# Routing with 18 small operations instead of 31, and GpSimd's scalings held until a turn's scores exist

## The chip, the cores and the metric

The kernel runs on one core of a Trainium2 chip. The metric is device time in microseconds (us), the median over runs. The core has several engines that work side by side, each through its own instructions in order: TensorE (PE, matmuls; PEld its weight loads), VectorE (DVE), ScalarE (ACT), GpSimd (POOL) and SyncE (SP), which here issues most transfers. They meet through semaphores: an instruction waits until others have got as far as it needs. Data lie in SBUF, and results of TensorE in the eight banks of PSUM.

## What is computed

A linear-attention layer (RWKV5) is followed by a mixture of experts with a cosine router, all in float32.

```python
B, H, S, D = 4, 8, 768, 48
for t in range(S):
    cur = einsum('bhd,bhe->bhde', u[None] * kt, vt)
    y[:, :, t] = einsum('bhd,bhde->bhe', rt, state + cur)
    state = w[None, :, :, None] * state + einsum('bhd,bhe->bhde', kt, vt)
x = y.transpose(0, 2, 1, 3).reshape(3072, 384)
# 8 experts, F = 1024
logits = (x / |x|) @ (emb / |emb|).T / tau
expert_idx = argmax(logits, axis=1)
gate_w = softmax(logits)[expert_idx]
for e in range(8):
    out[expert_idx == e] = gate_w * (relu(x @ w1[e]) @ w2[e])
```

Each of 3072 tokens goes to one expert. The router therefore makes, for each expert, a list of its tokens; the expert gathers those rows of x, and scatters its results.

## The kernel before

**Turns.** The sequence is cut into 6 chunks of 128 steps. A turn handles one chunk for two of the four batches (`u` = 0, 1), so there are 12 turns; turn t has chunk c = t // 2 and `bp` = t % 2. Within a chunk the recurrence becomes matmuls. GpSimd scales R and K by powers of the decay (`scale_r` L274, `scale_k` L270, tiles Rw and Kw), PE transposes them (`turn_in` L286), ACT copies them out of PSUM (`take_in` L290, tiles RT and KT). `scores` (L300) multiplies KT by RT into four banks D[0] to D[3], and DVE masks these into AT (`mask` L332). The diagonal gets its factor u from a second product: GpSimd makes KuT from KT (`own_k` L278), PE multiplies (`own_scores` L315), and DVE copies the diagonal into AT (`own_terms` L324). `outer` (L345) and `next_state` (L357) make the state after the chunk, `decay_state` (L363) scales it on GpSimd.

The outputs of a turn are made in the next one: `with_state` (L381) and `with_v` (L394) sum into banks Y[0] and Y[1], ACT copies them (`take_y` L401), PE transposes them into rows (`turn_y` L409), ACT copies the rows (`take_x` L413), SP stores them (`keep_x` L422), and ACT sums their squares (`squares` L428).

**Routing.** Every second turn a chunk is complete for all four batches. `logits` (L435) fills Y[0]; DVE copies it (`take_logits`), PE turns it (`turn_logits` L447), DVE copies it again (`keep_logits`). `choose_a` takes the root of the squares on GpSimd; `choose` (L469) divides the logits by the norm, finds the largest, makes a one-hot and running counts per expert; `exps` and `gate` make the weight; `ranks` (L505, PE) gives each token its rank among those of its expert, and `places` (L512), `places_b`, `put` and `collect` (L562) write its number and weight into that expert's list of up to 512. `choose`, `gate` and `places` have 31 small DVE operations a chunk. At the end `numbers_out` (L567) makes the list of row numbers, `take`.

**Order.** The order on every engine is written out by hand: `attention` (L579) gives each step a time within a plan, and the steps are emitted in the order of these times. They set nothing but the order, which all engines then follow. For turn t, `at` = t x PERIOD, `before` = a turn earlier, `nxt` = a turn later. Loads of K, R and V are planned three turns ahead on SP; the weights of the first two experts come on the same queue in turns 4 to 8.

**Experts.** After the turns, `experts` zeroes 8 row buffers G on GpSimd and gathers the rows of two experts into them (L665). Then for each expert PE transposes the rows (L678) and runs two layers (`layer1` L687, `layer2` L698).

The rest (`again`, `recur`, `slow_expert`) is for lists that overflow and for decays outside a range; it isn't entered with these inputs.

## Time and profile before

| | us |
|---|---|
| median of 3 runs | 576.18 |
| lowest and highest run | 575.48, 582.40 |
| the profiled execution | 575.27 |
| its span, first to last instruction | 573.4 |
| start of the first scores and of the last | 14.7, 176.9 |
| `take` ready | 206.2 |
| first matmul of the experts (L687) | 215.8 |

| engine | busy us | share |
|---|---|---|
| PE | 500.8 | 87% |
| PEld | 320.9 | 56% |
| DVE | 190.9 | 33% |
| POOL | 157.7 | 28% |
| ACT | 102.9 | 18% |

The profile is of one execution. The shares are over the whole span, of which the attention and routing take the first third and the experts the rest, so they say little on either stage. In the lists of the profile a row names the kernel's line, the engine, the operation and its tiles as out<-in, with partitions x elements; then the count and the time. A releaser is what an engine waited for.

### The profile page before, as it was taken

Reading aid. Unit: us, or ns where it says so; the run is one execution under the profiler, and the core shown is the slowest. Engines: PE = TensorE matmul, PEld = TensorE weight load, DVE = VectorE, ACT = ScalarE, POOL = GpSimd, SP = SyncE. Lnnn points to the kernel's source line nnn. Section 1 sums busy time; section 2 is a strip of 40 time slices with the busy share of each in tenths; the row PEclk is TensorE's granted clock in tenths of the full one; section 3 lists DMA queues with packets and bytes.
Section 4 is the critical chain, followed back from the end, with each engine's and each line's share of the span. In section 5 each row is a group of like instructions: output and inputs, shape, how many; then the busy total and the mean of one; then the engine's idle time right before and its main releaser. Section 6 shows DMA issues by size and latency. Waiting matters only on the chain.

```text
span 573.4 us, 9113 instructions
## 1 busy us (share of the span) xinstructions
PE 500.8 (87%) x3755; PEld 320.9 (56%) x3755; DVE 190.9 (33%) x423; ACT 102.9 (18%) x217; POOL 157.7 (28%) x186
## 2 busy tenths in 40 slices
PE   6799858597787639999999999999999999999990
PEld 3689757586776524554554554554554554554550
DVE  6576969779698520110110110110110110110001
ACT  2235503333043301101101101101101101101100
POOL 5676534535141244023023023023023020020020
PEclk9799969879699859999999999999999999999996
DMA  9966756937000112314314214314214213010010
GB/s 170 197 132 142 171 162 148 260 100 187 1 30 30 56 49 70 110 39 154 110 43 156 110 41 150 110 42 153 110 42 155 110 41 110 0 42 0 0 40 7
DMA packets 95510, 54.20 MB, mean 95 GB/s; under 512 B 78781, under 2 KB 90110, under 8 KB 95458
## 3 DMA queue, kind: packets, MB, share of 16 engines
q1 hardware_dynamic: 88658, 43.67, 27.9%
q0 software_dynamic: 4096, 9.45, 4.7%
q10 hardware_dynamic: 2704, 0.40, 0.4%
q8 instruction: 31, 0.51, 0.4%
q14 instruction: 21, 0.17, 0.1%
HBM read 45.63 MB, written 11.01 MB: 99 GB/s over the span
## 4 chain that ended last, share of the span: by engine, by line
PE 75%; DVE 15%; issue 2%; DMA 1%; ACT 0%; POOL 0%; DVEq 0%; POOLq 0%; ACTq 0%
PE ps L687 29%; PE po L698 29%; PE ps L300 4%; PE py L394 3%; PE py L381 2%; PE po L315 2%; PE py L678 2%; DVE AT L324 2%; PE ps L286 1%; DVE pre L488 1%; PE ps L345 1%; DVE xTe L679 1%; DVE P L549 1%; DVE oh L482 1%; DVE l L480 1%
## 5 line engine op out<-in xcount | busy, mean ns | idle before, releaser
L687 PE MATMUL ps<-xTe,w 128*128 128x512 f32 x384 | 166.5, 593 | 0.0
L698 PE MATMUL po<-w,hT 128*128 128x384 f32 x512 | 166.4, 486 | 0.0
L698 PEld LDWEIGHTS po<-w,hT 128*128 128x128 f32 x512 | 96.7, 190 | 66.2 <-issue 0.5
L687 PEld LDWEIGHTS ps<-xTe,w 128*128 128x128 f32 x384 | 73.1, 191 | 90.1 <-issue 88.3
L704 POOL DMA_INDIRECT out_dram<-y,take x32 | 31.7, 992 | 280.2 <-DVE y L703 276.1
L690 ACT ACTIVATE hT<-ps 128x512 f32<-128x512 f32 x64 | 38.2, 597 | 303.7 <-PE ps L687 303.7
L703 DVE TENSOR_SCALAR y<-po,lists 128x384 f32<-128x384 f32 x32 | 19.8, 618 | 165.5 <-PE po L698 165.5
L679 DVE COPY xTe<-py 128x512 f32<-128x512 f32 x24 | 15.9, 688 | 152.6 <-PE py L678 152.3
L324 DVE COPY_PREDICATED AT<-dmask,po 64x512 f32<-64x512 int32 x48 | 35.2, 734 | 8.3 <-PE po L315 7.6
L665 POOL DMA_INDIRECT G<-xs,take x32 | 32.6, 1020 | 18.4 <-DVE take L574 8.9
L300 PE MATMUL ps<-RT,KT 48*128 48x128 f32 x384 | 30.7, 322 | 6.6 <-ACT X L413 6.6
L332 DVE TENSOR_TENSOR AT<-ps,umask 128x512 f32<-128x512 f32 x48 | 30.0, 682 | 16.8 <-PE ps L300 16.8
L300 PEld LDWEIGHTS ps<-RT,KT 48*128 48x128 f32 x384 | 28.1, 229 | 9.2 <-ACT X L413 7.8
L401 ACT COPY YT<-py 128x512 f32<-128x512 f32 x24 | 12.9, 589 | 93.8 <-PE py L394 93.8
L363 POOL TENSOR_TENSOR T<-T,wC 128x384 f32<-128x384 f32 x10 | 8.3, 829 | 71.2 <-DVE inv L474 41.1
L278 POOL TENSOR_TENSOR KuT<-KT,uw 128x512 f32<-128x512 f32 x24 | 24.6, 1041 | 8.4 <-ACT KT L290 8.3
L274 POOL TENSOR_TENSOR Rw<-R,rpow 128x384 f32<-128x384 f32 x24 | 24.0, 1001 | 5.1 <-DVE wC L118 5.1
L394 PE MATMUL py<-AT,V 128*64 128x128 f32 x384 | 24.6, 283 | 0.0
L270 POOL TENSOR_TENSOR Kw<-K,kpow 128x384 f32<-128x384 f32 x24 | 24.2, 1010 | 0.0
L447 PE MATMUL py<-ident,lgT 128*128 128x128 f32 x6 | 2.4, 401 | 24.2 <-DVE lgT L443 24.2
L678 PE MATMUL py<-ident,G 128*128 128x128 f32 x96 | 15.6, 298 | 9.0 <-issue 5.2
L394 PEld LDWEIGHTS py<-AT,V 128*64 128x64 f32 x384 | 21.7, 142 | 1.1 <-issue 0.2
(152 smaller groups left out, 396.6 us busy)
## 6 DMA issues: line engine op xcount, KB each, us to landing
w<-in_moe_w_dram SPq DMA_DIRECT2D x24, 512.0 KB, 5.0
w<-in_moe_w_dram SPq DMA_DIRECT2D x32, 384.0 KB, 4.5
K<-in_k_dram SPq DMA_DIRECT2D x24, 192.0 KB, 3.4
V<-in_v_dram SPq DMA_DIRECT2D x24, 192.0 KB, 3.9
xs<-X SPq DMA_DIRECT2D x24, 192.0 KB, 2.1
R<-in_r_dram SPq DMA_DIRECT2D x22, 192.0 KB, 3.8
G<-xs,take POOLq DMA_INDIRECT x32, 3.6
out_dram<-y,take POOLq DMA_INDIRECT x32, 2.6
```

The lines of the kernel that those rows point to most:

```text
L270: k.nc.gpsimd.tensor_mul(of(k.Kw, t)[:, u, :, 0:D], of(k.K, t)[:, u], k.kpow)
L278: k.nc.gpsimd.tensor_mul(of(k.KuT, t)[:, u], of(k.KT, t)[:, u], k.uw[:, :, None].to_broadcast([128, NP, C]))
L300: k.nc.tensor.matmul(k.D[2 * u + par][:, p * C : (p + 1) * C], KT[rows, u, p, :], RT[rows, u, p, :], start=True, stop=True, skip_group_che ...
L324: k.nc.vector.copy_predicated(of(k.AT, t)[half, :, par].rearrange("q u (p i) -> q u p i", p=NP)[:, :, :, half], k.dmask[half, None, None, ...
L332: k.nc.vector.tensor_mul(of(k.AT, t)[:, u, par].rearrange("q (p i) -> q p i", p=NP), k.D[2 * u + par].rearrange("q (p i) -> q p i", p=NP), ...
L394: k.nc.tensor.matmul(y_out(k, par, p, u), V[:, u, 2 * p + par, :], AT[:, u, par, p * C : (p + 1) * C], start=c == 0 and u == 0 and q == 0, ...
L665: k.nc.gpsimd.indirect_dma_start(out=G[:, :], out_offset=None, in_=k.xs[:, :], in_offset=IndirectOffsetOnAxis(ap=k.take[:, e, t : t + 1], ...
L678: k.nc.tensor.transpose(ps[:, t * 128 : (t + 1) * 128], G[:, m * 128 : (m + 1) * 128], k.ident)
L687: k.nc.tensor.matmul(ps, w1[:, m, f * 128 : (f + 1) * 128], xT[:, m, :], start=(m == 0), stop=(m == NK - 1))
L690: k.nc.scalar.activation(hT[:, f, :], ps, ACT.Relu)
L698: k.nc.tensor.matmul(ps, hT[:, f, t * 128 : (t + 1) * 128], w2[:, f, :], start=(f == 0), stop=(f == NF - 1))
L704: k.nc.gpsimd.indirect_dma_start(out=k.out[:, :], out_offset=IndirectOffsetOnAxis(ap=k.take[:, e, t : t + 1], axis=0), in_=y[:, :], in_off ...
```

## The change

Seven things are edited.

1. `own_k` for the first half gets a dependency on the matmul of `scores` that was emitted last (`after`, `k.scored`). On GpSimd, in order, it stands ahead of the scalings for the next turn.
2. `choose` finds the largest among the logits as they are, and multiplies by the inverse norm only afterwards. The running counts over the four batches come from one scan over a tile `cum_oh` that holds the counts so far beside the one-hot; ACT copies the last count back. The small addition to the norm goes to GpSimd (`choose_a`).
3. `places` finds the tile of a rank by comparing it with 128, 256, 384, 512; the list's number and weight are laid side by side (`ng`), so that one product V of 32 elements and one QV of 256 take the place of Q and two QV of 128 each. V and QV move into `places_b`. `choose`, `gate`, `places` and V make 18 operations.
4. The lists start at SKIP, and numbers are stored less SKIP, so the last `collect` writes `take` itself; `numbers_out` goes.
5. The row buffers G are zeroed in turns 2 to 5.
6. The plan has other times: `own_k` after the scores of its own turn and not before, `decay_state` a turn later, `ranks` and `places` in the turn of `choose` and not in the next, `places_b`, `put` and `collect` in the turn after, where the next chunk's logits are made. The last two chunks have times of their own.
7. `turn_y` uses the banks D[0] and O[1] in this order, before O[1] and D[0]; `ranks` and `put` use other columns of Y[1].

```diff
-PERIOD = 10.0
+PERIOD = 11.2
...
+    k.ng = pool.tile([128, NCH, B, 2], F32, name="ng")
+    nc.vector.tensor_scalar_add(k.ng[:, :, :, 0], k.token, -float(SKIP))
...
+    k.level = numbers(k, "level", [128, TM], [[128, TM]], 128, 0)
+
+    k.cum_oh = pool.tile([128, E, B + 1], F32, name="cum_oh")
+    nc.vector.memset(k.cum_oh[:, :, 0:1], 0.0)
+    k.cum = k.cum_oh[:, :, 0]
+    k.oh = k.cum_oh[:, :, 1:].rearrange("q x b -> q b x")
+    k.on = pool.tile([128, E, B + 1], F32, name="on")
+    nc.vector.memset(k.on, 1.0)
+    nc.vector.memset(k.on[:, :, 0:1], 0.0)
+    k.back = pool.tile([128, NCH, B], F32, name="back")
+    k.rank = pool.tile([128, NCH, B], F32, name="rank")
+    k.lists = pool.tile([128, E, 2, TM], F32, name="lists")
+    nc.vector.memset(k.lists[:, :, 0, :], float(SKIP))
+    nc.vector.memset(k.lists[:, :, 1, :], 0.0)
+    k.take = pool.tile([128, E, TM], I32, name="take")
...
-    ps = k.bank[5].rearrange("q (g x) -> q g x", g=4)
+    ps = k.bank[1].rearrange("q (g x) -> q g x", g=4)
...
 def own_k(k, t, u):
-    k.nc.gpsimd.tensor_mul(
+    ins = k.nc.gpsimd.tensor_mul(
         of(k.KuT, t)[:, u], of(k.KT, t)[:, u], k.uw[:, :, None].to_broadcast([128, NP, C])
+    )
+    if u == 0:
+        after(k, ins, k.scored)
+
+
+def after(k, ins, other):
+
+    k.tc.add_manual_dep(
+        ins.ins, other.ins.name, mybir.DependencyInfo(mybir.DependencyClass.Sync, mybir.DependencyReason.DATA),
+        reason="turn",
     )
...
-            k.nc.tensor.matmul(
+            k.scored = k.nc.tensor.matmul(
...
 
 def choose_a(k, c):
+    ssq = k.ssq[c % 2]
+    k.nc.gpsimd.tensor_tensor(out=ssq, in0=ssq, in1=k.half, op=ALU.pow)
+    k.nc.gpsimd.tensor_scalar_add(ssq, ssq, 1e-6)
+
+
+def choose(k, c):
 
     nc, p = k.nc, k.rt
-    ssq = k.ssq[c % 2]
-    nc.gpsimd.tensor_tensor(out=ssq, in0=ssq, in1=k.half, op=ALU.pow)
-
-
-def choose(k, c):
-
-    nc, p = k.nc, k.rt
-    ssq = k.ssq[c % 2]
+    mx = p.tile([128, B], F32, name="mx", tag="mx")
+    nc.vector.reduce_max(mx, k.lg, axis=AX.X)
+    l = p.tile(FULL, F32, name="l", tag="l")
+    nc.vector.tensor_sub(l, k.lg, over_e(mx))
+    er = p.tile(FULL, F32, name="er", tag="er")
+    nc.vector.scalar_tensor_tensor(er, l, 0.0, k.rev[:, None, :].to_broadcast(FULL), ALU.is_equal, ALU.mult)
+    back = k.back[:, c, :]
+    nc.vector.reduce_max(back, er, axis=AX.X)
+    nc.vector.tensor_tensor(k.oh, er, over_e(back), ALU.is_equal)
+    k.counts = p.tile([128, E, B + 1], F32, name="counts", tag="counts")
+    flat = lambda a: a.rearrange("q x b -> q (x b)")
+    nc.vector.tensor_tensor_scan(flat(k.counts), flat(k.on), flat(k.cum_oh), 0.0, ALU.mult, ALU.add)
     inv = p.tile([128, B], F32, name="inv", tag="inv")
-    nc.vector.tensor_scalar_add(inv, ssq, 1e-6)
-    nc.vector.reciprocal(inv, inv)
-    l = p.tile(FULL, F32, name="l", tag="l")
-    nc.vector.tensor_mul(l, k.lg, over_e(inv))
-    mx = p.tile([128, B], F32, name="mx", tag="mx")
-    nc.vector.reduce_max(mx, l, axis=AX.X)
-    nc.vector.tensor_sub(l, l, over_e(mx))
-    oh = k.oh = p.tile(FULL, F32, name="oh", tag="oh")
-    nc.vector.scalar_tensor_tensor(oh, l, 0.0, k.rev[:, None, :].to_broadcast(FULL), ALU.is_equal, ALU.mult)
-    nc.vector.reduce_max(mx, oh, axis=AX.X)
-    nc.vector.tensor_tensor(oh, oh, over_e(mx), ALU.is_equal)
-    pre = k.pre = p.tile(FULL, F32, name="pre", tag="pre")
-    nc.vector.tensor_copy(pre[:, 0, :], k.cum)
-    for b in range(1, B):
-        nc.vector.tensor_add(pre[:, b, :], pre[:, b - 1, :], oh[:, b - 1, :])
-    nc.vector.tensor_add(k.cum, pre[:, B - 1, :], oh[:, B - 1, :])
+    nc.vector.reciprocal(inv, k.ssq[c % 2])
+    nc.vector.tensor_mul(l, l, over_e(inv))
     k.shifted = l
...
-    g = k.gates[:, c, :]
+    g = k.rt.tile([128, B], F32, name="g", tag="g")
     nc.vector.reduce_sum(g, k.shifted, axis=AX.X)
     nc.vector.tensor_scalar_add(g, g, 1e-9)
-    nc.vector.reciprocal(g, g)
+    nc.vector.reciprocal(k.ng[:, c, :, 1], g)
 
 
 def ranks(k, c):
     mm = k.nc.tensor.matmul
-    out = k.Y[1][:, 0 : B * E].rearrange("q (b x) -> q b x", b=B)
+    out = k.Y[1][:, 192 : 192 + B * E].rearrange("q (b x) -> q b x", b=B)
     mm(out, k.umask, k.oh, start=True, stop=False)
-    mm(out, k.ones, k.pre, start=False, stop=True)
+    mm(out, k.ones, k.counts[:, :, 0:B].rearrange("q x b -> q b x"), start=False, stop=True)
+    k.nc.scalar.copy(k.cum, k.counts[:, :, B])
...
+    full = p.tile(FULL, F32, name="full", tag="full")
+    nc.vector.tensor_mul(full, k.Y[1][:, 192 : 192 + B * E].rearrange("q (b x) -> q b x", b=B), k.oh)
+    r = k.rank[:, c, :]
+    nc.vector.reduce_sum(r, full, axis=AX.X)
+    wide = [128, B, TM]
+    over = p.tile(wide, F32, name="over", tag="over")
     nc.vector.tensor_tensor(
-        Q, k.slot[:, None, 0:width].to_broadcast(wide), e4[:, :, None].to_broadcast(wide), ALU.is_equal
-    )
-    k.QV = p.tile([128, B, 2, width], F32, name="QV", tag="QV")
-    nc.vector.tensor_mul(k.QV[:, :, 0, :], Q, k.number[:, c, :, None].to_broadcast(wide))
-    nc.vector.tensor_mul(k.QV[:, :, 1, :], Q, k.gates[:, c, :, None].to_broadcast(wide))
-    k.lo = lohi
+        over, r[:, :, None].to_broadcast(wide), k.level[:, None, :].to_broadcast(wide), ALU.is_ge
+    )
+    hi = p.tile([128, B], F32, name="hi", tag="hi")
+    nc.vector.reduce_sum(hi, over, axis=AX.X)
+    lo = k.lo = p.tile([128, B], F32, name="lo", tag="lo")
+    nc.vector.scalar_tensor_tensor(lo, hi, -128.0, r, ALU.mult, ALU.add)
+    nc.vector.tensor_tensor(
+        over, k.slot[:, None, 0:TM].to_broadcast(wide), hi[:, :, None].to_broadcast(wide), ALU.is_equal
+    )
+    k.at_tile = over
 
 def places_b(k, c):
-    P = k.P = k.rt.tile([128, B, 128], F32, name="P", tag="P")
+    nc, p = k.nc, k.rt
+    wide = [128, B, 2, TM]
+    V = p.tile(wide, F32, name="HV", tag="HV")
+    nc.vector.tensor_mul(
+        V, k.at_tile[:, :, None, :].to_broadcast(wide), k.ng[:, c, :, :, None].to_broadcast(wide)
+    )
+    wide = [128, B, E, 2 * TM]
+    k.QV = p.tile(wide, F32, name="QV", tag="QV")
+    nc.vector.tensor_mul(
+        k.QV, V.rearrange("q b j t -> q b (j t)")[:, :, None, :].to_broadcast(wide),
+        k.oh[:, :, :, None].to_broadcast(wide),
+    )
+    P = k.P = p.tile([128, B, 128], F32, name="P", tag="P")
...
+    new = k.Y[1][:, 128 : 128 + 2 * E * TM].rearrange("q (x j t) -> q x j t", x=E, j=2)
+    if c == NCH - 1:
+        k.nc.vector.tensor_add(k.take, k.lists[:, :, 0, :], new[:, :, 0, :])
+        k.nc.vector.tensor_add(k.lists[:, :, 1, :], k.lists[:, :, 1, :], new[:, :, 1, :])
+    else:
+        k.nc.vector.tensor_add(k.lists, k.lists, new)
...
-            plan.at(before + 0.0 + 2 * u, scale_r, k, t, u)
-            plan.at(before + 1.0 + 2 * u, scale_k, k, t, u)
+            plan.at(before + 3.0 + 2 * u, scale_r, k, t, u)
+            plan.at(before + 4.0 + 2 * u, scale_k, k, t, u)
             for which in range(2):
-                plan.at(before + 6.2 + 0.9 * u + 0.45 * which, turn_in, k, t, u, which)
-                plan.at(before + 6.6 + 1.2 * u + 0.6 * which, take_in, k, t, u, which)
-            plan.at(before + 8.0 + 1.1 * u, own_k, k, t, u)
+                plan.at(before + 7.4 + 1.4 * u + 0.45 * which, turn_in, k, t, u, which)
+                plan.at(before + 7.8 + 1.2 * u + 0.6 * which, take_in, k, t, u, which)
+            plan.at(at + 0.95 + u, own_k, k, t, u)
             plan.at(at + 0.9 * u, scores, k, t, u)
             for par in range(2):
                 plan.at(at + 1.0 + 1.4 * u + 0.7 * par, mask, k, t, u, par)
-        plan.at(at + 2.65, own_scores, k, t)
+        plan.at(at + 3.2, own_scores, k, t)
...
         if c < NCH - 1:
-            plan.at(at + 5.3, outer, k, t)
-            plan.at(at + 6.8, next_state, k, t)
-            plan.at(at + 7.2, decay_state, k, t)
-        plan.at(nxt + 1.75, with_state, k, t)
-        plan.at(nxt + 3.55, with_v, k, t)
+            plan.at(at + 6.4, outer, k, t)
+            plan.at(at + 7.4, next_state, k, t)
+            plan.at(nxt + 7.0, decay_state, k, t)
+        plan.at(nxt + 2.0, with_state, k, t)
+        plan.at(nxt + 4.4, with_v, k, t)
         for par in range(2):
-            plan.at(nxt + 5.3 + 0.6 * par, take_y, k, t, par)
+            plan.at(nxt + 6.4 + 0.6 * par, take_y, k, t, par)
         for u in range(2):
-            plan.at(nxt + 8.1 + 0.45 * u, turn_y, k, t, u)
-            plan.at(nxt + 9.1 + 0.6 * u, take_x, k, t, u)
-            plan.at(nxt + 9.2 + 0.6 * u, keep_x, k, t, u)
-            plan.at(nxt + 10.2 + 0.7 * u, squares, k, t, u)
-        if bp == 1:
-            plan.at(nxt + 9.0, logits, k, c)
-            plan.at(nxt + 9.5, take_logits, k, c)
-            plan.at(nxt + 9.8, turn_logits, k, c)
-            plan.at(nxt + 10.8, keep_logits, k, c)
+            plan.at(nxt + 9.7 + 0.45 * u, turn_y, k, t, u)
+            plan.at(nxt + 10.2 + 0.6 * u, take_x, k, t, u)
+            plan.at(nxt + 10.3 + 0.6 * u, keep_x, k, t, u)
+            plan.at(nxt + 11.4 + 0.7 * u, squares, k, t, u)
+        if bp == 1 and c < NCH - 1:
+            plan.at(nxt + 8.5, logits, k, c)
+            plan.at(nxt + 9.4, take_logits, k, c)
+            plan.at(nxt + 10.6, turn_logits, k, c)
+            plan.at(nxt + 10.9, keep_logits, k, c)
             then = nxt + P
+            plan.at(then + 2.9, choose_a, k, c)
+            plan.at(then + 7.9, choose, k, c)
+            plan.at(then + 9.3, exps, k, c)
+            plan.at(then + 9.72, ranks, k, c)
+            plan.at(then + 9.8, places, k, c)
+            plan.at(then + 11.0, gate, k, c)
+            last = 7.9 if c < NCH - 2 else 0.0
+            plan.at(then + P + last, places_b, k, c)
+            plan.at(then + P + (10.5 if c < NCH - 2 else 0.2), put, k, c)
+            plan.at(then + P + (11.0 if c < NCH - 2 else 0.3), collect, k, c)
+    end = NCH * 2 * P + 6.4
+    c = NCH - 1
+    plan.at(end + 1.3, logits, k, c)
+    plan.at(end + 1.4, take_logits, k, c)
+    plan.at(end + 5.0, turn_logits, k, c)
+    plan.at(end + 5.1, keep_logits, k, c)
+    plan.at(end + 5.9, choose_a, k, c)
+    for i, fn in enumerate((choose, exps, ranks, places, gate, places_b, put, collect)):
+        plan.at(end + 6.0 + i, fn, k, c)
     plan.at(-P + 0.4, load_small, k)
     plan.at(6.2, build_embeddings, k)
     plan.at(P + 6.2, decays, k)
+    for i, G in enumerate(k.G):
+        plan.at((2 + i // 2) * P + 7.5, k.nc.gpsimd.memset, G, 0.0)
     for e in range(2):
...
-    k.G = []
-    for i in range(8):
-        G = k.gp1.tile([128, DM], F32, name=f"G{i}")
-        nc.gpsimd.memset(G, 0.0)
-        k.G.append(G)
...
-    numbers_out(k)
...
-    n.rows, n.sums = (n.O[1], n.D[0]), n.D[0]
+    n.rows, n.sums = (n.D[0], n.O[1]), n.D[0]
...
+    n.G = [n.const.tile([128, DM], F32, name=f"G{i}") for i in range(2 * TM)]
```

## The prediction

> **What bounds the kernel now.** First the page: its span and the 40 slices of 14.3 us.
>
> ```profile
> span 573.4 us, 9113 instructions
> ...
> PE   6799858597787639999999999999999999999990
> ...
> DVE  6576969779698520110110110110110110110001
> ...
> POOL 5676534535141244023023023023023020020020
> PEclk9799969879699859999999999999999999999996
> ```
>
> From slice 15 on TensorE is full: the experts, whose instructions the change leaves as they are. Only the first 210 us can move, and there PE has holes, DVE is busiest, and the granted clock dips. So I cut that stretch at the starts of the scores (L300), 14.73, 26.81, 37.72, 48.20, 59.95, 78.46, 94.02, 112.87, 128.29, 147.13, 162.50 and 176.88, one per turn 0 to 11, and asked for busy time per engine. Columns: window and length, busy us and instructions of PE, PEld, DVE, ACT, POOL, then clock, DMA share, GB/s.
>
> ```profile
> 37.72:48.20 10.48, 10.00 (x217) 9.20 (x217) 6.19 (x10) 6.02 (x16) 8.64 (x10) 1.00 0.74 168
> ...
> 94.02:112.87 18.85, 11.81 (x253) 10.66 (x254) 16.91 (x35) 6.25 (x16) 10.39 (x11) 0.94 0.97 250
> 112.87:128.29 15.42, 14.12 (x225) 13.48 (x224) 10.25 (x19) 4.15 (x10) 3.97 (x5) 0.74 0.44 107
> ```
>
> Turn 2, without routing, takes 10.48 us. With routing a pair takes 34.3: in turn 6 DVE works 16.9 of 18.85 us, in turn 7 the clock is 0.74. The chain of waits says how:
>
> ```profile
> 108.58 0.93 DVE lohi L529
> ...
> 111.61 0.60 DVE P L549
> 112.21 0.21 DVE lgT L443
> 112.42 0.04 issue
> 112.47 0.47 PE py L447
> 112.94 3.72 PE ps L300 x32
> ```
>
> `places` runs ahead of the logits copy on DVE, `turn_logits` waits behind it on PE (6.1 us idle), and the scores then run at half clock: 3.72 us against 1.99 at 48.27. The timeline shows why DVE is slow:
>
> ```profile
> 125.15 2.04 POOL L278 TENSOR_TENSOR KuT<-KT,uw 128x512 f32<-128x512 f32 x2 [0.19 <-ACT KT L290]
> 125.25 0.98 DVE L480 TENSOR_TENSOR l<-l,mx 128x32 f32<-128x32 f32 x1
> ...
> 126.27 0.96 DVE L482 SCALAR_TENSOR_TENSOR oh<-l,rev 128x32 f32<-128x32 f32 x1
> 127.27 0.19 DVE L483 TENSOR_REDUCE mx<-oh 128x4 f32<-128x32 f32 x1
> ```
> ```profile
> 184.79 0.19 DVE L480 TENSOR_TENSOR l<-l,mx 128x32 f32<-128x32 f32 x1
> 185.02 0.20 DVE L482 SCALAR_TENSOR_TENSOR oh<-l,rev 128x32 f32<-128x32 f32 x1
> ```
>
> At 185 us, GpSimd idle, the same two operations take a fifth: beside a GpSimd scaling each ends when the scaling ends. Reductions (0.19) and operations that read PSUM are not held (the 48 masks span 0.67 to 0.69).
>
> **The change, part by part.** S is the end of a turn's scores and S+2.2 means 2.2 us later; durations are those of before's rows, with its 0.1 from one engine's end to another's start.
>
> *The hold.* `own_k` now waits for the last score emitted before it. Its plan time at+0.95 comes after both halves of the scores (at and at+0.9), so it waits for all of them. Behind it on GpSimd stand its second half, the next turn's four scalings and the decay: KuT to S+1.1 and S+2.2 (1.04 each), the scalings 0.967 apart to S+6.1, decay to 6.9. In odd turns the power (1.02) and the new add (unseen; between 0.1, the small memset, and 1.0, the power; I take 0.3, being plain arithmetic) come ahead of the scalings: 7.4 and 8.2. `own_scores` waits for KuT: it ends at S+2.75 instead of S+1.95, cost 0.8 per turn, nothing hiding it. `own_terms` follows to 2.85+3.0=5.9, `next_state` to 6.5.
>
> *Even turn.* Now PE leads. After 2.75 it runs, by the starts in turns 3 and 8 of before, `with_v` 1.9, `outer` 0.92, `turn_in` 1.74, `logits` 1.05+0.17, `turn_y` 0.87, `put` 0.85, `turn_logits` 0.35, scores 2.0: S+12.6, and 0.3 for gaps of 0.1, so a turn of 12.9. DVE runs `places_b` from 6.5: at most 0.5 waiting for the decay, V 0.2 (32 elements), QV 0.4 (256 elements, between 0.29 for 128 and 0.68 for 512), P 0.68: done by 8.4, while PE is in `logits`; `put` starts at 9.3. So 0.9 of cover; each us beyond it would lengthen the turn by one. The logits copy (0.28) follows and is done before `put` ends.
>
> *Odd turn.* Now DVE and ACT lead. `choose` starts at 6.5: maximum 0.2; `l` ends with the last scaling, 7.4; `er` with the decay, 8.3; then GpSimd is through, and `back`, `oh`, `inv`, `l` take 0.2 each, the scan 0.3 (40 elements; the row with 512 took 1.23, the plain small ones 0.17): 9.4. `ranks` and the second `turn_y` on PE wait for the scan, done by 10.1. ACT's queue holds `exps` ahead of the last KT copy, and behind that the new `cum` copy and `take_x`: 0.25+0.6+0.2+0.5, so D[0] is free for the scores at 11.0, and the turn is 13.0. PE alone would need 11.2. `places` (six, 1.3) and `gate` (0.65) fit before the first mask at 12.0. With the add at 1.0 an odd turn is 13.7, at 0.1 12.8. If `choose` were held throughout, its last three would add 2.4.
>
> *The 31 routing operations become 18.* Of the old ones some fifteen a pair are held for 0.6 to 1.0; of the new ones two or three. The sums above contain this. What is late next is `own_terms`, then `take_x`. PE's longest wait becomes about 1.1 us, so I use the warm durations throughout.
>
> *Banks and queues.* `turn_y` now fills D[0] first, so the scores no longer wait for the second `take_x`: that wait, 1.3 to 2.15 us on L413, goes in even turns. `keep_x`'s two transfers move with `take_x`; the loads behind them on SP are for three turns on, a lead of some 39 us against the 0.8 to 4.2 that two of them take. `decay_state` moves a turn back on GpSimd; its state is read two turns on.
>
> *Start.* Turn 0 pays the hold dearly. Scores end at 16.7, KuT at 18.9 (before 16.55), scalings 22.8, embedding's power 23.4 and memset 23.9, then on DVE the scaled embedding to 24.5, on PE its transposes 25.2, DVE 25.9, PE 26.4. `outer` and all of `turn_in` stand behind these on PE, on a cold clock (four took 1.06 at 24.97): 31.0 for the next scores, against 26.81. Turn 1, with `decays` (1.55) ahead of the last `own_terms`, gives 11.2; turn 2, 11.75; turn 3 is odd, 13.0.
>
> *Sum.* Turn lengths after: 16.3, 11.2, 11.75, 13.0, then 12.9 and 13.0 three times, 12.0 for turn 10 (no `outer`): 141.95. Before: 162.15. Gain 20.2, being minus 7.1 up to turn 4 and plus 27.3 later.
>
> *Tail.* Now 29.3 us from the start of the last scores to the end of `take` (206.19). After it: `own_terms` to S+5.9, `choose` 1.75, `places` 1.3, `gate` 0.65, V to P 1.35 give 11.1; `put` 1.0 to 1.97, `collect` 0.3; only then `with_state` (same bank) 1.05, `with_v` 1.9, `take_y` 0.9, `logits` 1.2, `turn_y` 0.9, logits turned and copied 0.55: 19.1 to 20.0. The squares (1.44 behind `take_x` 1.0) and the power hold `inv` to 22.1 or 23.0; then `l` 0.2, `places` 1.3, `gate` 0.65, V to P 1.35, `put`, and `take` straight from the last `collect` 0.3 (the two operations of `numbers_out`, 0.4, are gone): S+27.8 to 28.8. With the scores' 2.06, and the middle: 30.4, so 1.1 lost. It gains little from 18 operations because with GpSimd idle the old ones cost 0.2 each here already, and because `put` of chunk 4 now stands ahead of `with_state`. The gathers are unchanged; their zeroing, 3.0 on GpSimd before, was hidden and now runs after the decay, in turns 2 to 5. Memsets don't hold DVE (0.19 beside them at 196 us).
>
> *A rule against the change.* No tensor-with-scalar operation runs on GpSimd before. The Trainium skill (GPSIMD Engine Reference, 2.1 Instruction dispatch) says that the first call to a freshly loaded kernel costs about 6 us, unseen in the profile. Here the first tensor-tensor at 10.19 took 1.01, like the rest, and the first affine select 0.29. By the rule turn 3 grows by 6 and the time is 563; by the rows nothing. I take nothing and keep 6 for the range.
>
> Net 20.2-1.1=19.1. The profiled execution took 575.27 (573.4 and 1.9 around it): 556.2. The median of the runs is 0.9 above it, so 557.
>
> **Rivals.**
> *Deeper (0.13).* `choose` is not held (minus 1.6 per odd turn), and stray gaps close: turns of about 12, 9 us more, 548. For it: GpSimd is free for the last 5 us of a turn. Against: the ACT order is fixed.
>
> *Clock and queue (0.16).* Waits in odd turns add up. 2.15 us idle at 57.8 left the scores at 2.06; 6.1 made them 3.72. The skill (TensorE: Matmul & The Clock Gate, Part 1) puts the fall at an idle window of about 3.4 us, free-running. If one more held operation (1.0) is enough, scores, `with_state`, `own_scores` lose 1.7+0.9+0.9 four times, with the 4 us waited: 18 back, 575. By 1.1 us waits neither row nor rule expects it.
>
> *GpSimd becomes the bound (0.08), slower.* Masks and `own_terms` now run beside KuT and the scalings in every turn. If these held GpSimd as its scalings hold DVE, seven operations would each wait about 0.7, the turn's loop (KuT 2.2, power 1.3, scalings 3.9, transposes 0.5, copy 0.6, scores 2.0, 0.4 of handoffs: 10.9) becomes 15.8, eleven of them 174, and with the start 178: 592. It decides from a mean turn of 14.6 up. Against it: at 28.6 to 32.5 the scalings kept 0.97 beside masks and copies.
>
> *Transfers (inside the ranges).* Their share is 0.97 in turns 4 and 6, but turns 4 to 9 sum to 59 us of transfer (length by share) in what will be 78.
>
> **How the numbers follow.** Forecast 0.63, 550 to 566; the add and the 6 us are in it. 2% is 11.5 us, about what a measurement here tells from no change: faster is under 564.7. Faster 0.13+0.57=0.70, same 0.06+0.16=0.22, slower 0.08. Leaving out 1 in 10 above and below: 546 to 577.
>
> **What would show it.** Right: score starts near 31, 67, 93, 119, 145, 157; first KuT of a turn 0.1 after its last score; `l` and `er` at 0.7 to 1.0 and the rest of `choose` at 0.2; clock 1.00 in turns 5, 7, 9; `take` near 187. Wrong: pairs well off 25.9, scalings longer than 1.0, scores at 3.7.

## The result, and the profile after

| | before | after |
|---|---|---|
| median of 4 runs, us | 579.29 | 560.94 |
| lowest and highest | 575.48, 584.99 | 560.64, 562.14 |
| the profiled execution | 575.27 | 561.12 |
| its span | 573.4 | 559.3 |
| start of the first scores and of the last | 14.7, 176.9 | 15.8, 159.5 |
| `take` ready | 206.2 | 191.6 |
| first matmul of the experts | 215.6 | 200.4 |

The ratio is 0.971 with a 95% interval of 0.964 to 0.978: faster. It leaves out runs that lie more than 1.5% above the fastest of the same kernel, here the 584.99 of before. The forecast was 557.0. The 215.6 is the first record of L687; the 215.8 given earlier is where the chain enters that row. From here on a line number is that of the kernel whose profile is shown; in the changed kernel `own_k` is L286, `scores` L318, `own_scores` L333, `choose` L490 to L503.

First the page of the changed kernel: the span, and the rows of PE, DVE and the clock in 40 slices of 14.0 us.

```profile
span 559.3 us, 9057 instructions
...
PE   7588998989897389999999999999999999999990
...
DVE  6545667685772310200200110110110110100001
...
PEclk9788999999996679999999999999999999999996
```

The clock no longer dips in the middle of the turns. What is left of half clock lies at the start (second to fourth digit) and in the tail (13th to 15th).

The stretches of turns 2, 7 (odd) and 8 (even), cut at the starts of the scores; columns as in the prediction, that is length, busy us of PE, PEld, DVE, ACT, POOL, then clock, DMA share, GB/s:

```profile
45.01:58.66 13.65, 11.94 (x218) 10.89 (x218) 6.29 (x11) 5.17 (x13) 7.38 (x9) 0.87 0.53 116
109.46:122.19 12.73, 11.02 (x222) 9.62 (x221) 9.74 (x25) 4.68 (x14) 7.96 (x9) 1.00 1.01 262
122.19:134.84 12.65, 12.09 (x257) 10.97 (x257) 8.16 (x18) 5.75 (x15) 6.69 (x7) 1.00 0.70 163
```

A pair of turns with routing takes 25.4 us where it took 34.3, and DVE works 17.9 us in it where it worked 27.2. In the even turn PE stands idle for 0.56 us only.

The chain of what ended last, through the odd turn 7 (start, length, engine, tile and line):

```profile
111.69 2.05 POOL KuT L286 x2
...
113.79 0.77 PE po L333 x32
...
118.26 0.83 DVE l L492
...
119.12 0.76 DVE er L494
...
121.08 0.07 ACT KT L308
...
121.75 0.39 ACT X L431
...
122.19 2.10 PE ps L318 x32
```

It goes from the held KuT over `own_scores`, the `own_terms` on DVE (left out here), `choose` and ACT's queue to `take_x`, which frees D[0] for the next scores. `l` and `er` are still held beside GpSimd's scalings, as the old operations were; everything after them in `choose` takes 0.15 to 0.24.

### The profile page after: what moved, and what is told of

Same layout as the page of the kernel before. It is cut to its first block, busy times and chain, and to the rows that moved or that the text cites. A ratio compares the mean times of both kernels' runs of the same rounds, so it can differ in the third digit from the quotient of the medians.

```text
span 559.3 us, 9057 instructions
## 1 busy us (share of the span) xinstructions
PE 502.6 (90%) x3755; PEld 316.6 (57%) x3755; DVE 154.1 (28%) x352; ACT 103.5 (19%) x223; POOL 158.8 (28%) x191
## 3 DMA queue, kind: packets, MB, share of 16 engines
q1 hardware_dynamic: 88658, 43.67, 28.2%
## 4 chain that ended last, share of the span: by engine, by line
PE 77%; POOL 7%; DVE 6%; issue 3%; ACT 1%; DMA 1%; POOLq 0%; ACTq 0%; DVEq 0%
PE ps L706 30%; PE po L717 30%; POOL KuT L286 4%; PE ps L318 4%; PE py L412 3%; PE ps L304 2%; DVE AT L342 2%; PE py L697 2%; PE py L572 1%; PE po L333 1%; PE py L453 1%; PE ps L363 1%; DVE xTe L698 1%; POOL Rw L282 1%; POOL Kw L278 1%
## 5 line engine op out<-in xcount | busy, mean ns | idle before, releaser
L286 POOL TENSOR_TENSOR KuT<-KT,uw 128x512 f32<-128x512 f32 x24 | 24.5, 1040 | 64.6 <-PE ps L318 61.1
L350 DVE TENSOR_TENSOR AT<-ps,umask 128x512 f32<-128x512 f32 x48 | 29.8, 683 | 15.8 <-PE ps L318 15.8
L318 PE MATMUL ps<-RT,KT 48*128 48x128 f32 x384 | 25.1, 281 | 3.0 <-ACT X L431 2.8
L412 PE MATMUL py<-AT,V 128*64 128x128 f32 x384 | 26.6, 297 | 0.0
L419 ACT COPY YT<-py 128x512 f32<-128x512 f32 x24 | 12.9, 589 | 71.0 <-PE py L412 71.0
L318 PEld LDWEIGHTS ps<-RT,KT 48*128 48x128 f32 x384 | 22.8, 190 | 5.6 <-ACT X L431 4.4
L333 PE MATMUL po<-RT,KuT 48*64 48x64 f32 x768 | 16.7, 224 | 9.8 <-POOL KuT L286 9.8
L412 PEld LDWEIGHTS py<-AT,V 128*64 128x64 f32 x384 | 23.5, 150 | 1.1 <-issue 0.4
L333 PEld LDWEIGHTS po<-RT,KuT 48*64 48x64 f32 x768 | 13.4, 134 | 14.3 <-POOL KuT L286 14.3
```

What stands on the lines that cost most here:

```text
L286: ins = k.nc.gpsimd.tensor_mul(of(k.KuT, t)[:, u], of(k.KT, t)[:, u], k.uw[:, :, None].to_broadcast([128, NP, C]))
L318: k.scored = k.nc.tensor.matmul(k.D[2 * u + par][:, p * C : (p + 1) * C], KT[rows, u, p, :], RT[rows, u, p, :], start=True, stop=True, ski ...
L333: k.nc.tensor.matmul(k.O[par][half, col : col + DP], KuT[rows, u, p, half], RT[rows, u, p, half], start=True, stop=True, skip_group_check= ...
L350: k.nc.vector.tensor_mul(of(k.AT, t)[:, u, par].rearrange("q (p i) -> q p i", p=NP), k.D[2 * u + par].rearrange("q (p i) -> q p i", p=NP), ...
L412: k.nc.tensor.matmul(y_out(k, par, p, u), V[:, u, 2 * p + par, :], AT[:, u, par, p * C : (p + 1) * C], start=c == 0 and u == 0 and q == 0, ...
```

## The experiments

Each kernel was run together with the kernel before on the same chip; a ratio is to that kernel. Medians of different groups are only as good as those ratios, so where two variants are close the traces decide. Where a row is given for a variant, the diff is against the changed kernel unless it says otherwise.

**1. The change without the hold.**

```diff
-    if u == 0:
-        after(k, ins, k.scored)
```

> The changed kernel without the dependency of own_k on the scores; everything else as changed. Theory A, the hold earns its wait by keeping GpSimd off the routing: KuT then starts as soon as KT is copied, which in the changed kernel's odd turns is in the middle of choose and places; if each of its two halves holds two of their operations by 0.8 us, an odd turn grows by about 3 us less the 0.8 that own_scores gains, and the time is 566 or more. Theory B, the hold costs more than it brings: own_scores ends 0.8 us earlier in all turns, even turns have 0.9 us of cover on DVE, and the time is 552 to 558.

Measured: 546.22 (543.30 to 549.22), ratio 0.946 [0.939, 0.954]. Its interval lies wholly below that of the changed kernel. The hold is a cost, of about 14 us (14.7 by the medians, 13.9 by the spans of the profiles), and the time is below even the 552 to 558 that were expected if it costs something. A GpSimd row of turn 8 in this variant, then the same kernel's clock over turns 3 to 9 (its starts of scores 49.79 and 131.20):

```profile
116.31 1.05 POOL L286 TENSOR_TENSOR KuT<-KT,uw 128x512 f32<-128x512 f32 x1 [3.36 <-ACT KT L306]
```
```profile
49.79:131.20 81.41, 76.03 (x1651) 71.18 (x1652) 64.70 (x146) 36.84 (x93) 54.83 (x64) 1.00 0.80 201
```

KuT for the next turn is made as soon as ACT has copied KT, inside the turn before. `own_scores` then follows the scores without a wait, and the seven turns average 11.63 us against 12.73. `choose` is mostly free too (`l` and `er` 0.19 each in turn 7). What is held now are single operations: `lo` of `places` 0.71 to 1.05, one of `gate` 0.77, QV once, 1.15; on these nothing waits. In turns 3 and 9 it is the scan, 1.02 and 1.00, and there `ranks` waits 0.48 for it.

**2. The hold for the second half lifted.** GpSimd now waits for the first half of the scores only, about 1 us earlier.

```diff
-            k.scored = k.nc.tensor.matmul(
+            ins = k.nc.tensor.matmul(
...
+            if u == 0:
+                k.scored = ins
```

> The changed kernel with own_k held only until the first half of the turn's scores exists, 1.0 us earlier. If the wait of own_scores for KuT (0.26 and 0.30 us, and with it all of GpSimd's chain) sets the length of every turn, turns shorten by 0.7 to 1.0 and the time is 550 to 554. If DVE sets it otherwise (own_terms can't start before the masks end, S+1.7), or KuT then meets the gate operations, it is 558 to 561.

Measured: 547.45 (546.17 to 548.46), ratio 0.948 [0.943, 0.954]: nearly all of the first variant's gain, more than either number expected. The odd turn 7 in its timeline:

```profile
103.28 2.04 POOL L286 TENSOR_TENSOR KuT<-KT,uw 128x512 f32<-128x512 f32 x2 [6.11 <-PE ps L318]
104.83 1.23 PE L335 MATMUL po<-RT,KuT 48*64 48x64 f32 x64
109.86 0.79 DVE L494 TENSOR_TENSOR l<-lg,mx 128x32 f32<-128x32 f32 x1
110.68 0.75 DVE L496 SCALAR_TENSOR_TENSOR er<-l,rev 128x32 f32<-128x32 f32 x1
```

In the changed kernel the same matmuls come in two runs with a wait before each:

```profile
112.79 0.69 PE L333 MATMUL po<-RT,KuT 48*64 48x64 f32 x32 [0.26 <-POOL KuT L286]
113.79 0.69 PE L333 MATMUL po<-RT,KuT 48*64 48x64 f32 x32 [0.30 <-POOL KuT L286]
```

So most of the price of the hold is TensorE's wait for KuT, and not the slow `choose`: `l` and `er` are as slow here as with the full hold, and freeing them in experiment 1 brings turns 3 to 9 another 0.43 each. PE's waits for KuT fall from 9.8 us to 2.0 in all. Turns 3 to 9 average 12.06, 0.67 less than with the full hold; that is 4.7 us. Another 6.3 come in turns 0, 1, 2 and 10, above all 2.5 in turn 2 and 1.8 in turn 0, where the clock had been low.

**3. New operations alone.** The changed kernel's routing and early zeroing, with the order, banks and plan of before, and no hold:

```diff
-PERIOD = 11.2
+PERIOD = 10.0
...
-            plan.at(then + 9.72, ranks, k, c)
-            plan.at(then + 9.8, places, k, c)
-            plan.at(then + 11.0, gate, k, c)
...
+            plan.at(then + P + 0.9, gate, k, c)
+            plan.at(then + P + 8.0, ranks, k, c)
+            plan.at(then + P + 8.6, places, k, c)
```

> The new routing operations and early zeroing, in the old order of a turn, with the old banks and no hold. Theory A, removing operations alone is most of the gain: choose falls from 7.3 to about 4.5 us and places from 7.7 to about 5, a pair from 34.3 to about 29, and the time is 557 to 563. Theory B, what matters is where the GpSimd scalings lie, for the operations left are held as the old ones were and the clock still falls in each pair: 567 to 574.

Measured: 570.84; the four runs took 558.27, 568.22, 573.46 and 573.84, and no ratio was formed. The fastest lies below every run of the changed kernel. PE of the run profiled, the one of 573.46, around the end of turn 6:

```profile
116.99 0.48 PE L463 MATMUL py<-ident,lgT 128*128 128x128 f32 x1 [3.60 <-DVE lgT L459]
```

The shorter `places` still stands ahead of the logits copy, and PE still waits for it, 3.6 us instead of 6.1; DVE's operations there are held (`P` 1.47, QV 1.15). In this order fewer operations shorten the wait but don't remove it: at the ends of turns 4, 6, 8 and 10 it is 3.91, 3.60, 3.59 and 1.54 (before: 6.1 after turn 6, 2.70 after turn 10). How much they bring alone is not settled.

**4. New order alone.** The changed kernel's plan, banks and hold with the 31 old operations; `gate` stands ahead of `places`:

```diff
-            plan.at(then + 11.0, gate, k, c)
+            plan.at(then + 9.75, gate, k, c)
```

> The new order, banks, hold and early zeroing with the 31 old routing operations (gate stands ahead of places, which the old operations need). Theory A, the operations count: choose has five more at 0.2 and one or two more held, places nine more and two wide ones, an odd turn is about 3.5 us longer than 12.7 and the tail about 5, the time 575 to 580. Theory B, the order is most of the gain: the old operations cost 0.2 each once GpSimd is out of their way and hide beside PE, 564 to 568.

Measured: 572.94, from runs of 564.42, 572.87, 573.01 and 573.58, against 575.95 for before in the same group; no ratio was formed here either. In the profile, of the run of 572.87, odd turns take 12.6 as in the changed kernel, the even turns 6 and 8 take 14.8 instead of 12.65. PE between turn 5 and 6:

```profile
96.43 0.41 PE L518 MATMUL py<-oh,umask 128*128 128x32 f32 x2 [0.86 <-DVE oh L494]
...
97.92 2.98 PE L310 MATMUL ps<-RT,KT 48*128 48x128 f32 x32
```

The old `choose` costs the odd turn nothing. It makes `ranks` wait longer, and after that the scores run on a falling clock (2.98), with_state takes 1.96 and own_scores 1.93. Up to the last scores this variant lies 7.1 us behind the changed kernel, and its tail is 4.8 longer (36.9 us from the start of the last scores to `take`, against 32.1).

By the medians of the groups either half alone gives 3 to 5 us; together they give 18, and without the hold 30. But the medians of 3 and 4 can't carry this: their runs lie 15 and 9 us apart, and by the fastest runs (575.25 for before) the halves give 17 and 11. What the operations bring and what the order brings is not parted.

**5. The kernel before, kept warm.** To part the clock from the wait itself, this kernel leaves the wait before `turn_logits` where it was and fills most of it with matmuls (diff against before):

```diff
+def fill(k, count):
+    for i in range(count):
+        k.nc.tensor.matmul(k.D[1][:, 0:128], k.ones, k.ones, start=True, stop=True, skip_group_check=True)
...
+            if 1 <= c <= 3:
+                plan.at(nxt + 9.79, fill, k, 23)
             plan.at(nxt + 9.8, turn_logits, k, c)
```

> The kernel before, with 23 filler matmuls (ones by ones, 128 wide, some 5.3 us, into D[1]) ahead of turn_logits for chunks 1 to 3, in the 6 to 7 us in which TensorE waits for the logits copy behind places. The wait itself stays. It asks how much of what the change gained was clock, and how much the wait. Theory clock: scores of turns 5, 7 and 9 fall from 3.8 to 2.1, with_state from 1.96 to 1.1, own_scores from 1.93 to 1.1, with_v from 2.3 to 2.0, 4.6 us a pair: 560 to 565. Theory wait: what follows in the odd turn is paced by VectorE, beside which TensorE's slower matmuls were hidden: pairs stay at 33 to 34 and the time at 572 to 577.

Measured: 571.68 (570.31 to 573.78), ratio 0.987 [0.978, 0.997]. The time is just beside the second theory's numbers, but the pairs agree better with the first, which had 4.6 us a pair. Before's pair of turns 6 and 7, then that of this variant:

```profile
94.02:128.29 34.27, 25.93 (x477) 24.14 (x477) 27.15 (x54) 10.41 (x26) 14.36 (x16) 0.85 0.73 186
```
```profile
93.08:123.56 30.48, 27.45 (x524) 25.79 (x524) 26.96 (x54) 10.42 (x26) 14.39 (x16) 1.00 0.80 209
```

The next pair takes 34.21 and 30.47. At clock 1.00 a pair takes 30.5: so of the 8.9 us by which the change shortened a pair, 3.8 were clock; the other 5.1 are the wait and DVE's work and whatever else the order changed, not parted further. In the first pair the fillers ended 1.5 us before the logits came, the clock fell all the same, and only 0.8 was gained. And 3.4 us went again in the tail, which leads to the row below (before, then this variant, at the start of the last scores, where neither has a filler):

```profile
176.62 0.33 PE L447 MATMUL py<-ident,lgT 128*128 128x128 f32 x1 [2.70 <-DVE lgT L443]
176.88 2.06 PE L300 MATMUL ps<-RT,KT 48*128 48x128 f32 x32
```
```profile
168.17 0.33 PE L447 MATMUL py<-ident,lgT 128*128 128x128 f32 x1 [2.71 <-DVE lgT L443]
168.43 3.79 PE L300 MATMUL ps<-RT,KT 48*128 48x128 f32 x32
```

The same wait, after the same work: once the scores run at full clock, once at half. What differs is where the wait lies on a grid. In each of the 13 profiles the granted clock changes only at whole multiples of 3.41 us after its first change (144 changes in all, to 0.003 us), and where this grid lies against the start of the kernel differs from run to run. Cut on it, before's wait is shared by two stretches, and this kernel's falls into one:

```profile
172.05:175.46 3.41, 1.87 (x40) 1.44 (x38) 2.83 (x14) 2.51 (x8) 2.48 (x3) 1.00 0.33 118
175.46:178.87 3.41, 2.25 (x34) 2.01 (x34) 2.02 (x7) 0.00 (x0) 0.21 (x1) 1.00 0.00 0
```
```profile
165.01:168.42 3.41, 0.70 (x20) 0.32 (x9) 2.86 (x13) 1.09 (x4) 1.27 (x2) 1.00 0.31 115
168.42:171.84 3.42, 3.42 (x33) 3.42 (x32) 1.43 (x3) 0.00 (x0) 0.00 (x0) 0.50 0.02 5
```

PE was busy for 1.87 and 2.25 us of 3.41 in before, and the clock stayed; here for 0.70, and the clock was halved in the next stretch.

**6. The tail, filled, with too much.** 20, 12, 34 and 30 fillers, ahead of the put of chunk 4, the last ranks, the last put, and the transposes of the gathered rows:

```diff
+    plan.at(NCH * 2 * P + 0.15, fill, k, 20)
+    plan.at(end + 7.9, fill, k, 12)
+    plan.at(end + 11.5, fill, k, 34)
+    plan.at(end + 13.5, fill, k, 30)
```

> The changed kernel with filler matmuls (ones by ones, 128 wide, into a PSUM bank that is free by then) put in TensorE's queue in the tail: 20 ahead of the put of chunk 4, 12 ahead of the last ranks, 34 ahead of the put of chunk 5, 30 ahead of the first transposes of the gathered rows. Nothing else is changed. Theory: the tail and the first expert layer are longer than forecast because TensorE's clock has fallen to half there; kept busy, put of chunk 4 and of chunk 5 take about 1.0 each instead of 1.97, with_state 1.1 instead of 2.33, with_v 2.0 instead of 3.60, logits 1.1 instead of 1.34, and the first expert layer 21.0 instead of 22.3: together 5 to 6 us, so 555 to 556. Rival: the waits of the tail (P for the put, the gathered rows) end last whatever the clock is, and the fillers are no gain or are themselves in the way: 560 to 563.

Measured: 565.86 (565.08 to 567.29), ratio 0.981 [0.975, 0.987]: not faster than the changed kernel. The rival was right for this kernel: the fillers were themselves in the way. A filler runs as two matmuls of 0.115, so they were twice as long as the waits (PE's timeline):

```profile
173.74 4.63 PE L579 MATMUL ps<-ones 128*128 128x128 f32 x40
178.21 1.00 PE L572 MATMUL py<-QV,P 128*128 128x64 f32 x8
```

But `put` does take 1.00 now, and with_v 1.97. The tail is 33.7 us instead of 32.1. The other 4.0 of the profile are no cost of the fillers: the last scores start that much later than in the changed kernel, after turns with the same instructions, with more half clock at the start and in turn 10.

**7. The tail, filled with half as many** (11, 6, 17 and 15 fillers at the same places).

> The changed kernel with the same fillers in the tail, but about half as many: 11, 6, 17 and 15 in place of 20, 12, 34 and 30. In the first version each filler took two passes of 0.115, so that 20 took 4.6 us in a wait of 2.6, and 34 took 7.8 in a wait of 4.1; now they are 2.5, 1.4, 3.9 and 3.5. Theory (half clock is what the tail lost): put, with_state, with_v and put again lose 1.0+0.9+1.6+1.0, so the list of rows is ready some 4 us earlier than in the changed kernel, counted from the last scores (28 in place of 32.1), and the time is 556 to 558. Rival: the fillers only move the wait to another place, the list comes 31 to 32 after the last scores and the time is 560 to 562.

Measured: 558.11 (555.73 to 560.26), ratio 0.962 [0.953, 0.971]. By the ratios alone this can't be told from the changed kernel; by the trace the tail can. The changed kernel's tail, then this one's:

```profile
172.52 1.97 PE L572 MATMUL py<-QV,P 128*128 128x64 f32 x8 [2.63 <-DVE P L564]
174.42 2.33 PE L399 MATMUL py<-RT,T 48*48 48x128 f32 x32
176.68 3.60 PE L412 MATMUL py<-AT,V 128*64 128x128 f32 x32
...
189.42 1.97 PE L572 MATMUL py<-QV,P 128*128 128x64 f32 x8 [4.13 <-DVE P L564]
```
```profile
176.33 1.10 PE L572 MATMUL py<-QV,P 128*128 128x64 f32 x8 [0.17 <-DVE P L564]
177.37 1.47 PE L399 MATMUL py<-RT,T 48*48 48x128 f32 x32
178.77 1.97 PE L412 MATMUL py<-AT,V 128*64 128x128 f32 x32
...
190.00 1.10 PE L572 MATMUL py<-QV,P 128*128 128x64 f32 x8 [0.28 <-DVE P L564]
```

From the last scores to `take` it is 28.0 us, which is the theory's number; the changed kernel has 32.1. The first expert layer takes 21.6 instead of 22.5. So some 5 us of the changed kernel's tail and first layer are half clock.

**8. Embeddings ahead of turn 0's scalings.**

```diff
-    ps = k.bank[1].rearrange("q (g x) -> q g x", g=4)
+    ps = k.bank[7].rearrange("q (g x) -> q g x", g=4)
...
-    plan.at(6.2, build_embeddings, k)
+    plan.at(0.93, build_embeddings, k)
```

> The changed kernel with build_embeddings planned at 0.93 instead of 6.2 in turn 0, its second bank being bank 7; the hold stays. Theory: turn 0 is 17.1 long because the embeddings' two GpSimd steps stand in GpSimd's queue behind the two held scalings of turn 0 and the next turn's scalings behind them; put ahead of the scalings, the scores of turn 1 start at 25 to 29 instead of 32.9 and the kernel takes 554 to 558. Rival: turn 0 waits for the arrival of turn 1's rows and for the small loads, not for the embeddings: scores of turn 1 stay at 32 to 33 and the time at 560 to 562.

Measured: 555.98 (555.00 to 560.79), ratio 0.966 [0.958, 0.974]. The scores of turn 1 start at 28.99, so turn 0 takes 12.34 and not 17.09, though its first scores come 0.9 later: the queue behind the hold is what had made turn 0 long. Turn 2 is unchanged (13.6).

**9. No hold, and a filled tail.** First with the long fillers (20, 12, 34, 30), then with the halved ones, then with 4 more ahead of the scores of turn 10:

```diff
+    plan.at(10 * P - 0.01, fill, k, 4, 1)
```

> The changed kernel without the hold and with the same fillers in the tail. Theory (two separate losses, the hold in the turns and the half clock in the tail): their gains add, so about 5 below the kernel without the hold, 540 to 543. Rival: without the hold the tail is paced by other things, and the fillers bring under 2: 544 to 547.

> The kernel without the hold, with the halved fillers in the tail. Theory: as without the hold (546) less 3 to 4 from the tail: 541 to 544. Rival: no gain, 545 to 547.

> The kernel without the hold and with the halved fillers in the tail, and 4 more fillers (0.9 us, into D[1]) ahead of the scores of turn 10, where TensorE waits 0.86 for take_x. In that kernel's profile the scores of turn 10 took 3.41, and turn 10 took 15.5 against 11.5 to 12 in the turns around it. Theory: that wait of 0.86, with the 0.48 before it, is what drops the clock; filled, the scores of turn 10 take 2.06, the turn 12 or less, and the time is 541 to 542. Rival: the clock falls there for the gaps earlier in the turn, or at the next wait: scores of turn 10 stay above 2.8 or those after it are slow, and the time stays at 544 to 546.

Measured: 548.49 (544.67 to 549.58), ratio 0.950 [0.942, 0.957]; 545.14 (538.44 to 545.65), ratio 0.937 [0.927, 0.948]; and 538.03 (537.45 to 539.23), ratio 0.934 [0.932, 0.936]. The first misses, for the reason found in 6. The second gains in the tail (28.2 against 31.0 without the hold), but its profile shows half clock in turn 10, which takes 15.5. The third, four matmuls longer, does in turn 10 what its theory said: the scores take 2.06 and the turn 10.7; the tail is 27.0, and the four runs lie within 1.8 us. Its median is 7 us lower than the second's, but the two ran on different chips, and their ratios can't be told apart; what the fillers bring there is read from the trace. PE ahead of those scores in the second and in the third:

```profile
132.43 3.41 PE L316 MATMUL ps<-RT,KT 48*128 48x128 f32 x32 [0.86 <-ACT X L429]
```
```profile
129.12 1.06 PE L577 MATMUL ps<-ones 128*128 128x128 f32 x8
130.15 2.06 PE L316 MATMUL ps<-RT,KT 48*128 48x128 f32 x32
```

This is the lowest median of all, 6.6% below before.

## Why the prediction was right, and where it missed

The forecast's own sum, against the changed kernel's profile; a plus is time gained:

| term | forecast | measured |
|---|---|---|
| first scores | 0 | -1.05 |
| turns 0 to 3 | -7.0 | -10.4 |
| turns 4 to 10 | +27.2 | +28.8 |
| last scores to `take` | -1.1 | -2.8 |
| `take` to the first expert matmul | 0 | +0.6 |
| experts | 0 | -1.1 |
| sum | +19.1 | +14.1 |

(The forecast's own turn lengths give the -7.0 and +27.2 used here; it wrote 7.1 and 27.3.) So 5 us less was gained than forecast. That the medians of the two groups of runs differ by 18.4, nearly the forecast gain, is luck: the median of before was 579.29 in this group and 576.18 when the forecast was made.

**The steady turns: right, step by step.** Even 12.9 forecast, 12.65 measured, PE leading; odd 13.0 forecast, 12.73 measured, and through the very chain that was named. After the end of the scores at 111.5, `l` ended at S+7.6 (forecast 7.4), `er` at S+8.4 (8.3), and D[0] came free at S+10.6 (11.0). The scan took 0.24, QV 0.43, P 0.68. The clock was 1.00 from turn 3 to turn 9.

**The hold: right in kind and size, missed in its reach.** 0.8 a turn was forecast as a wait on PE that nothing hides; experiment 2 takes 0.67 a turn away in turns 3 to 9, and experiment 1 takes 1.1, since it also frees `choose`. With turn 0, 4.2 longer than before, the forecast had some 12 us for it; removing it brings about 14. What the forecast missed is the clock: "PE's longest wait becomes about 1.1 us, so I use the warm durations throughout". That is the step that failed, in two ways: PE's waits became longer (1.3 in turns 0 to 2, and 2.6 and 4.1 in the tail), and waits of 1.3 and 0.3 close together were enough to halve the clock. In turn 2 (PE's rows, then two stretches of the grid of experiment 5):

```profile
48.34 0.69 PE L333 MATMUL po<-RT,KuT 48*64 48x64 f32 x32 [1.27 <-POOL KuT L286]
49.34 0.69 PE L333 MATMUL po<-RT,KuT 48*64 48x64 f32 x32 [0.30 <-POOL KuT L286]
49.96 3.34 PE L412 MATMUL py<-AT,V 128*64 128x128 f32 x32
```
```profile
46.94:50.36 3.42, 1.84 (x76) 1.52 (x74) 2.09 (x5) 0.00 (x0) 3.12 (x4) 1.00 1.04 205
50.36:53.77 3.41, 3.41 (x44) 3.41 (x42) 2.65 (x4) 0.86 (x2) 3.41 (x4) 0.50 0.43 87
```

Both waits for KuT fall into one stretch of the grid, and in the next the clock is 0.50: with_v took 3.34 instead of 1.97, and turn 2 was 13.65, not 11.75. The clock falls at this place in all five profiles with the full hold (the changed kernel and experiments 4, 6, 7 and 8), and in none of the others. Turn 1 was 0.9 too short as well (12.14 against 11.2); 0.24 of that are scores on the half clock, the rest wasn't followed.

**Turn 0: right in kind, 0.8 too short** (17.09 against 16.3). The scalings and the embeddings queued behind the hold as told; the first scores took 2.25 and PE's work after the embeddings ran at clock 0.50. Experiment 8 shows that the embeddings' place in the queue is worth 4.75 us of this turn.

**The tail: the same step.** `put`, with_state, with_v and the second `put` measured 1.97, 2.33, 3.60 and 1.97. The forecast had 1.0 to 1.97, 1.05, 1.9 and 1.97: it allowed for half clock in `put` alone. Experiment 7 brings the tail from 32.1 to 28.0 with nothing but fillers. Of the experts' 1.1, 0.9 is the first layer on half clock, 22.5 against 21.6 filled.

**First scores, 1.05 late: the clock, before anything that was edited.** The first twelve matmuls (L89) are the same in both kernels; they end at 8.61 in before, where the clock rises at 4.80, and at 9.19 in the changed kernel, where it rises at 5.98. The rest are transposes of `turn_in` that take 1.1 there instead of 0.66. The first scores start at 14.6 to 14.7 in before and in experiment 5 and at 15.4 or later in the other eleven profiles; why the clock rises later in all of these stays open.

**The unseen add** took 0.23 in all six places, the first at 64.0 included; 0.3 had been taken between 0.1 and 1.0. The 6 us of the Trainium skill (GPSIMD Engine Reference, 2.1) for a first call do not show, as the prediction's rows had it.

**The rivals.** GpSimd as the bound fell: its scalings kept 0.95 to 0.97 from one to the next beside the masks. The deeper rival's 12 us turns do exist, but only with half of the hold or none. The clock rival, 575, had the right mechanism in a smaller dose: it looked for it in the odd turns, where waits of up to 0.86 left the clock at 1.00, while with_v of turn 2 (1.4), the tail (4.1) and the first layer (0.9) paid.

**What made the change faster.** Of a pair's 8.9 us, 3.8 are the clock that fell in the wait behind `places`; the other 5.1 are that wait, DVE's held work and the rest of the new order. In the profiles neither the 18 operations nor the order does it alone: in the old order a wait of 3.6 us stays, and with the old operations the ranks come later and the even turns run on a falling clock. But one run of the operations alone took 558.27, so this is not shown for every run. The new use of the banks was not tried by itself. The hold takes back nearly half of what the rest gives.

## What to carry to other kernels

A wait added to keep an engine out of another's way has to be priced at the instruction that waits for that engine, here TensorE's second product, and on everything queued behind it in the first turns; letting it end 1 us earlier, after half of the scores, got back nearly all. Where TensorE's waits add up to more than 1 us within any 3.41 us, price the matmuls that follow from both clocks: the length of the wait doesn't say which of them holds, since the place of the grid isn't known beforehand. Filler matmuls no longer than the wait took 4.1 us out of the tail. Measure a filler before counting it: at twice the length of the waits the gain in the tail became a loss of 1.6.

## What the hardware showed that was not expected

- The clock fell in turn 2 of the changed kernel after a stretch of 3.41 us with waits of 1.27 and 0.30, and in the no-hold kernel with filled tail after one with 0.48 and 0.86. The Trainium skill (TensorE: Matmul & The Clock Gate, Part 1) puts the fall at an idle window of about 3.4 us; the length of the window agrees with the grid here, but PE was busy for 54% and 61% of these two, and the measurements decide.
- In the 13 profiles PE's busy share of a stretch goes with what follows. Of the stretches at full clock, those with PE busy for 70% or more were never followed by a fall (0 of 1789, most of them in the experts), those under 45% nearly always (46 of 47), those between in 26 of 56.
- So the same wait doesn't always have the same result: 2.70 us left the scores at 2.06 in before and 2.71 made them 3.79 in experiment 5. And 0.86 ahead of turn 10 left them at 2.06 in the changed kernel and made them 2.77 and 2.86 in experiments 6 and 7, whose turns up to there have the same instructions: PE was busy for 75% of the stretch with this wait in the first, and for 69% and 68% in the other two.
- Once low, the clock stayed at 0.50 from 172.5 to 180.0 in the changed kernel, with PE busy 7.48 of these 7.5 us. In turn 2 it was low for one stretch only, 50.36 to 53.77, also with PE busy throughout; what decides how long it stays low is not shown.
- With one wait of 0.86 filled, the four runs lay 1.8 us apart instead of 7.2, with the median at the lowest of the runs without it (538.0 and 538.4). That the clock's falls are most of such a spread fits this, but with four runs of each it is not shown.
